# mLSTM scores as 64x64 quadrants, k in 128 rows, and one PSUM bank for all logits

## The chip, the cores and the metric

The kernel runs on one core of one Trainium2 chip. The metric is the device time of one execution in microseconds. Matmuls run on TensorE (PE, with PEld for the loads of its weights), elementwise work on VectorE (DVE), ScalarE (ACT) and GpSimd (POOL), and most DMAs are issued by SyncE (SP). A matmul writes PSUM, which has 8 banks of 512 float32 columns in 128 rows.

## The reference

An mLSTM layer with 4 batches, 8 heads, 768 positions and head size 40 gives x; a mixture of 8 experts, top 1, is applied to x. Everything is float32.

```python
for t in range(S):                      # C: [B,H,40,40], n: [B,H,40], m: [B,H]
    m_new  = max(f[t] + m, i[t])
    f_s, i_s = exp(f[t] + m - m_new), exp(i[t] - m_new);  m = m_new
    C = f_s * C + i_s * outer(v[t], k[t]);  n = f_s * n + i_s * k[t]
    y[t] = sigmoid(o[t]) * (C @ q[t]) / max(abs(n . q[t]), 1)
x = y as [3072 tokens, 320]
logits = normalize(x) @ normalize(expert_emb).T / tau
e, gate = argmax(logits), softmax(logits)[argmax]
out = gate * (relu(x @ w1[e]) @ w2[e])  # w1: [8,320,1024], w2: [8,1024,320]
```

## The kernel before

The recurrence is computed in chunks of L = 64 positions. One step n of the main loop (line 1290, NS = 24 steps) takes one batch and P = 128 positions, two chunks c, for all 8 heads. The heads are split as 4 pairs (index a, NP = 4) of two (index r). A chunk needs its scores (k against q, masked), the state that it starts from, and the product of scores and values. Loads of q, k and the rows of k and v come for two steps at a time (a pair q of steps, NS // 2 = 12 pairs, NB = 3 buffers).

In step n of the loop, TensorE gets its work in this order: `stage_add(n, 0)` (L664 adds the old state by an identity matrix, L674 adds the first chunk's keys times values); `stage_scores(n + 1)` (L637); now and then part of the routing; `stage_y(n)` (L712 scores times values, L725 q times state, and between them in odd steps the five transposes of L792); `stage_add(n, 1)`; in odd steps the router's logits of two steps (L812, two matmuls of 2 x E = 16 columns for each of 5 blocks of 64 features). ScalarE copies the state in the middle of the step from PSUM to `c_mid` in `stage_mid` (L690), which stands right behind `stage_add(n, 0)`. The state in PSUM and y share one bank: `pcv` and `yv` are two parts of the tile `y`. VectorE masks the scores of step n + 1 in `stage_weigh` (L646), and POOL scales the values in `stage_uv` (L622).

The scores of a step are 2 chunks x 4 pairs x 2 heads = 16 products of k and q over 40 rows, each issued as two matmul instructions. q has the even pair's 40 rows in partitions 0 to 39 and the odd pair's in 64 to 103, zeros between. k has two tiles: `k_e` holds the even pairs in the lower half and zeros in the upper, `k_o` the odd pairs in the upper half and zeros in the lower. Each product runs over all 128 rows; the zeros take the other pair out. The zeros are written once per buffer: by VectorE and POOL for buffer 0 (L1095, 1096, 1103, 1109), by ScalarE in `zero_act` (L1087) for buffers 1 and 2. The two heads r of a pair go to the two halves of PSUM's rows, r * 64; all scores of a step fill one bank (tile `s`, pool `pS`).

Loads are issued on SP's queue in the order of the loop: in an even step `stage_k` for a whole pair (two DMAs of 40 rows, L601), in an odd step `stage_q` for a whole pair (one of 128 rows, L607), each followed by `stage_row` (L595) and `stage_sig` (L615), from step 10 on by loads of the first experts' weights (`raw`, L173 to L184), and at the end of the step by the store of x of an earlier step (`x_d`, L766). In some steps ScalarE rounds a piece of those weights (L197), between its other work.

The router works on three groups of steps, GROUPS = (0, 6), (6, 14), (14, 24). Each group has its own PSUM tile `pm`, of the pool `pM` with two buffers. In it lie the logits, the ranks of the tokens within each expert (`pmv(g, 1)`), the sums that give the lists of tokens (`pids`) and counts (`cntv`). The order of the routing is the table `ROUTE` (line 1038); its VectorE parts wait in `vq` and are taken out one at a time by `tick`.

PSUM in the loop: pX 1 bank, pM 2, pY 3, pS 1, pJ 1. After the loop the banks of pY, pS and pJ go to the experts' pools pH and pO; the first experts' x is transposed by `x_tile` into banks of pS and pM, and `x_chunk` takes turns between pM and pX. The order of all work is written out by hand (`manual_schedule`).

Of the kernel before, what the change touches and what calls it, by code (L numbers as in the profile page):

```python
# [11 lines left out]
F32 = mybir.dt.float32  # L12
# [11 lines left out]
E, F = 8, 1024  # L24
# [42 lines left out]
def tile_mlstm_moe(  # L67
# [148 lines left out]
    pX = mctx.enter_context(tc.tile_pool(name="pX", bufs=1, space=PSUM))  # L216
    pM = mctx.enter_context(tc.tile_pool(name="pM", bufs=2, space=PSUM))

# [88 lines left out]
    pp, banks = [], []  # L307
    turns = [(pM, "pm"), (pX, "px")]

# [228 lines left out]
    with ExitStack() as actx:  # L538
# [6 lines left out]
        ap = ictx.enter_context(tc.tile_pool(name="ap", bufs=2, side="right"))  # L545
        pS = ictx.enter_context(tc.tile_pool(name="pS", bufs=1, space=PSUM, side="right"))
        pJ = ictx.enter_context(tc.tile_pool(name="pJ", bufs=1, space=PSUM, side="right"))


# [22 lines left out]

        k_e, k_o, q_s, kv_s, kr_s, vr_s, uv, w_s = [], [], [], [], [], [], [], []
        for i in range(NB):
            k_e.append(ap1.tile([P, 2, NP, P], F32, name=f"k_e{i}"))
            k_o.append(ap1.tile([P, 2, NP, P], F32, name=f"k_o{i}"))
            q_s.append(ap1.tile([P, 2, NP, P], F32, name=f"q_s{i}"))
            kv_s.append(ap1.tile([P, 2, 2, NP, D + D1], F32, name=f"kv_s{i}"))
            kr_s.append(kv_s[i][:, :, :, :, 0:D])
            vr_s.append(kv_s[i][:, :, :, :, D:])  # L580
            uv.append(ap1.tile([P, 2, NP, 2, D1], F32, name=f"uv{i}"))
            w_s.append(ap1.tile([P, 2, NP, L], F32, name=f"w_s{i}"))
        c_st = [ap1.tile([P, NP, 2 * D1], F32, name=f"c_st{b}") for b in range(B)]
# [15 lines left out]
        def stage_k(q, ks=slice(0, 2)):  # L599
            for r, kk in ((0, k_e), (1, k_o)):  # L600
                SY.dma_start(  # L601
                    kk[q % NB][r * L : r * L + D, ks].rearrange("d n a t -> d (n a t)"),
                    kt[q, r][:, ks].rearrange("d n a t -> d (n a t)"),
                )

# [23 lines left out]
        def stage_scores(n):  # L629
            q, k = divmod(n, 2)  # L630
            s = st.setdefault(n, {})["s"] = pS.tile([P, 2, NP, L], F32, name=f"s_{n}", tag="ps")
            for c in range(2):
                cs = slice(c * L, c * L + L)
                for a in range(NP):
                    for r in range(2):
                        m = a // 2 * 2 + r
                        T.matmul(  # L637
                            s[r * L : r * L + L, c, a],
                            (k_e, k_o)[a % 2][q % NB][:, k, m, cs],
                            q_s[q % NB][:, k, m, cs],  # L640
                            start=True,
                            stop=True,
                        )

        def stage_weigh(n):
            V.tensor_tensor(  # L646
                w_s[n % NB].rearrange("p c a t -> p (c a) t"),
                st[n]["s"].rearrange("p c a t -> p (c a) t"),
                late.unsqueeze(1).broadcast_to([P, 2 * NP, L]),
                ALU.mult,  # L650
            )
# [53 lines left out]
        def stage_y(n, mid=None):  # L705

            q, k = divmod(n, 2)
            y = st[n]["y"]
            yp = y[:, 0 : H * D1].rearrange("p (a q r d) -> p a q r d", a=NP // 2, q=2, r=2)
            for a in range(NP):  # L710
                for c in range(2):
                    T.matmul(  # L712
                        y[c * L : c * L + L, a * 2 * D1 : (a + 1) * 2 * D1],
                        w_s[n % NB][:, c, a],
                        uv[n % NB][:, c, a].rearrange("p r d -> p (r d)"),
                        start=False,
                        stop=n < B and c == 0,
                        skip_group_check=True,
                    )
            if mid:  # L720
                mid()
            for m in range(NP):
                for c, state in ((0, c_st[n % B]), (1, c_mid[n % 2])):
                    if n >= B or c:
                        T.matmul(  # L725
                            yp[c * L : c * L + L, m // 2, :, m % 2],
                            q_s[q % NB][:, k, m, c * L : c * L + L],
                            state[:, m].rearrange("p (q d) -> p q d", q=2),
                            start=False,
                            stop=True,  # L730
                            skip_group_check=True,
                        )
# [68 lines left out]
        def stage_logits(q):  # L801
# [3 lines left out]
            b = n - GROUPS[g][0]  # L805
            if b == 0:
                grp[g] = dict(pm=pM.tile([P, 512], F32, name=f"pm_{g}", tag="pm"))
            xt = st.pop(n)["xt"]
            st.pop(n + 1)
            for c in range(NX):  # L810
                for r0 in (0, L):
                    T.matmul(  # L812
                        grp[g]["pm"][r0 : r0 + L, b * E : (b + 2) * E],
                        xt[:, c, r0 : r0 + L],
# [21 lines left out]

        def pmv(g, k):
            w = nt(g) * E
            return grp[g]["pm"][:, k * w : (k + 1) * w].rearrange("p (t e) -> p t e", e=E)

        def pids(g):
            return grp[g]["pm"][:, 2 * nt(g) * E : 2 * nt(g) * E + E * NTT]

# [3 lines left out]
        def route_a(g, n0=0, n1=None):  # L847
# [3 lines left out]
            mx = sm(g, f"mx{n0}", [P, n])  # L851
            pl = pmv(g, 0)[:, n0:n1]
            V.tensor_reduce(mx, pl, AX.X, ALU.max)
# [72 lines left out]
        def route_rank(g):  # L926

            n, rkp, oh = nt(g), pmv(g, 1), ohg(g)
            T.matmul(rkp, tri, oh, start=True, stop=False)
# [6 lines left out]
        def route_b(g):  # L936
# [3 lines left out]
            ro = sm(g, "ro", [P, n, E])  # L940
            V.tensor_tensor(ro, pmv(g, 1), oh, ALU.mult)
            yield
# [61 lines left out]
        def cntv(g):  # L1004
            return grp[g]["pm"][:, 3 * P : 3 * P + E]

# [74 lines left out]

        def flat(t):
            return t.rearrange("p n a t -> p (n a t)")

        def zero_act(t):

            A.activation(  # L1087
                flat(t).rearrange("p (g t) -> p g t", t=P),
                onef.unsqueeze(1).broadcast_to([P, 2 * NP, P]),
                AF.Copy,  # L1090
                scale=0.0,
            )

        fill(FILLS[0])
        V.memset(k_e[0][:, 0], 0.0)  # L1095
        G.memset(k_o[0][:, 0], 0.0)
        stage_gates(1, A)
# [4 lines left out]
        V.memset(onef, 1.0)  # L1102
        V.memset(k_e[0][:, 1], 0.0)
        V.memset(ones[:, 1:], 1.0)
# [3 lines left out]
        G.memset(c_mid[0], 0.0)  # L1108
        G.memset(k_o[0][:, 1], 0.0)
        G.memset(uv[1], 0.0)  # L1110
        G.memset(c_mid[1], 0.0)
        zero_act(k_e[1])
        stage_k(0, slice(1, 2))
# [17 lines left out]
        A.activation(u0, gi[0:NH, 0], AF.Exp, bias=na0)  # L1131
        zero_act(k_o[1])
        fill(FILLS[1])
# [127 lines left out]
        def embeddings(k):  # L1261
# [3 lines left out]
            elif k == 1:  # L1265
# [4 lines left out]
                V.tensor_scalar(en, en, ens, taub[:E], ALU.mult, ALU.mult)  # L1270
                zrow = flat(k_e[2])[P - 1 : P]
                SY.dma_start(x_d[PAD : PAD + 1], zrow[:, 0:DM])
# [17 lines left out]
        for n in range(NS):  # L1290
            last = n == NS - 1
            q = (n + 4 - n % 2) // 2
            if n and q < NS // 2:
                (stage_q if n % 2 else stage_k)(q)
            if q < NS // 2:
# [189 lines left out]
        work(1, 0)  # L1485
        stage_xts(n // 2, pM, "pm")
        do(1)
# [4 lines left out]
        double(xs_a[:, 1], 0, HALF)  # L1492
        x_tile(xa[1], xs_a[:, 1], 0, pM, "pm")
        stage_sq(n - 1)
# [96 lines left out]
    hs = hidden("b")  # L1591
    banks += [(pH, "ph")] * 2 + [(pM, "pm")] * 2
    for e in range(NE):
# [212 lines left out]
def _layout(q, k, v, i_gate, f_gate, o_gate, moe_expert_emb, moe_tau, moe_w1, moe_w2):  # L1806
# [24 lines left out]
    def by_token(a):  # L1831
# [38 lines left out]
```

## Time and profile before

| what | us |
|---|---|
| median of 3 runs | 326.04 (324.49 to 328.71) |
| the profiled execution | 328.47 |
| its span, first to last instruction | 326.7 |
| busy in the span: PE / PEld | 307.4 / 290.8 |
| busy in the span: DVE / ACT / POOL | 217.2 / 164.1 / 146.4 |
| scores (L637): matmuls on k_e and on k_o | 2 x 384 instructions, 222 to 223 ns each |
| c_mid (L690) on ACT | 48 copies, 293 ns each |

Times in the profile are microseconds from the start of the span. An instruction's duration on PE includes its way through the array, so two that start close together overlap; what a block costs is read from the start of its first instruction to the start of the next block. The chain of waits goes back from the last instruction to whatever released each piece of work. The loop over the 24 steps fills the first 112 us or so, the experts the rest.

### The profile page before, as it was taken

How to read it: one execution, taken by the hardware profiler on the slowest of the kernel's cores; microseconds unless marked ns; L12 is line 12 of the kernel's file. 1: busy time of each engine (PE TensorE's matmuls, PEld its weight loads, DVE VectorE, ACT ScalarE, POOL GpSimd, SP SyncE). 2: the span in 40 equal slices, each digit the busy share in tenths (PEclk: the TensorE clock that was granted, in tenths of full speed). 3: DMA queues.
4: the chain of work that ended last, by engine and by line, in shares of the span. 5: the costliest groups of instructions: out<-in, count | busy, mean ns of one | idle time of the engine just before them, and what ended most of it. 6: DMA issues, size and time to landing. Idle time of an engine off the chain costs nothing.

```text
span 326.7 us, 9770 instructions
## 1 busy us (share of the span) xinstructions
PE 307.4 (94%) x3769; PEld 290.8 (89%) x3769; DVE 217.2 (66%) x631; ACT 164.1 (50%) x431; POOL 146.4 (45%) x182
## 2 busy tenths in 40 slices
PE   8998999989988879999999999999999999999991
PEld 3787999978876779999999999999999999999990
DVE  5776797897775549796567684574585584766520
ACT  4656556655663695344265463263373463555300
POOL 6659777688784297040635302321251321512121
PEclk9999999999999979999999999999999999999998
DMA  7998797998997523030594964446446465411001
GB/s 228 283 342 252 264 306 238 290 321 272 340 340 219 183 55 113 2 80 3 180 328 168 316 187 134 129 131 191 124 105 247 112 198 198 129 48 42 10 26 33
DMA packets 25101, 58.52 MB, mean 179 GB/s; under 512 B 3707, under 2 KB 10056, under 8 KB 25046
## 3 DMA queue, kind: packets, MB, share of 16 engines
q1 hardware_dynamic: 22166, 48.91, 47.0%
q0 software_dynamic: 2624, 8.48, 8.4%
q8 instruction: 31, 0.51, 0.7%
q10 hardware_dynamic: 256, 0.43, 0.4%
q14 instruction: 24, 0.20, 0.2%
HBM read 49.98 MB, written 8.19 MB: 178 GB/s over the span
## 4 chain that ended last, share of the span: by engine, by line
PE 84%; DVE 4%; DMA 4%; ACT 4%; issue 2%; POOL 1%; POOLq 0%; DVEq 0%; ACTq 0%
PE ph L390 29%; PE po L428 17%; PE s L637 4%; PE po_b L428 4%; PE po_a L428 4%; PE y L712 4%; PE y L674 3%; PE y L725 3%; PE po L415 3%; PE pt L351 2%; PE warm L1078 2%; DMA k_o<-in_kt 2%; PE pm L812 2%; PE px L792 2%; DMA raw<-in_w 2%
## 5 line engine op out<-in xcount | busy, mean ns | idle before, releaser
L447 POOL DMA_INDIRECT out<-ob,ids x20 | 20.3, 1015 | 99.2 <-DVE ob L444 73.7
L622 POOL TENSOR_TENSOR uv<-kv_s,u_t 64x328 f32<-64x328 f32 x47 | 35.3, 751 | 12.7 <-PE y L674 5.4
L428 PE MATMUL po<-w2h,hh 128*128 128x320 f32 x128 | 40.3, 315 | 0.0
L392 ACT ACTIVATE hh<-ph 128x448 fp32r<-128x448 f32 (+2 forms) x48 | 23.7, 493 | 32.7 <-PE ph L390 29.8
L428 PE MATMUL po<-w2h,hl 128*128 128x320 f32 x128 | 39.6, 309 | 0.0
L428 PE MATMUL po<-w2l,hh 128*128 128x320 f32 x128 | 39.5, 309 | 0.0
L394 DVE SCALAR_TENSOR_TENSOR hl<-ph,hh 128x384 fp32r<-128x384 f32 (+1 forms) x48 | 24.5, 511 | 14.6 <-ACT hh L392 12.3
L390 PE MATMUL ph<-xh,w1l 128*128 128x448 f32 (+2 forms) x96 | 32.0, 337 | 0.0
L390 PE MATMUL ph<-xh,w1h 128*128 128x448 f32 (+2 forms) x96 | 32.0, 336 | 0.0
L197 ACT CAST w1h<-raw 128x512 fp32r<-128x512 f32 x48 | 28.9, 616 | 5.4 <-DMA raw<-in_w 4.9
L444 DVE TENSOR_SCALAR ob<-po,gts 128x320 f32<-128x320 f32 x16 | 8.8, 551 | 27.8 <-PE po L428 27.8
L200 DVE TENSOR_TENSOR w2l<-raw,w2h 128x320 fp32r<-128x320 f32 x58 | 26.7, 497 | 0.2
L197 ACT CAST w2h<-raw 128x320 fp32r<-128x320 f32 x64 | 26.1, 461 | 0.0
L637 PE MATMUL s<-q_s,k_e 128*64 128x64 f32 x384 | 24.5, 223 | 1.2 <-DVE w_s L646 1.2
L690 ACT COPY c_mid<-y 40x164 f32<-40x164 f32 x48 | 14.0, 293 | 22.0 <-PE y L674 21.6
L637 PE MATMUL s<-q_s,k_o 128*64 128x64 f32 x384 | 24.5, 222 | 0.5 <-issue 0.5
L390 PE MATMUL ph<-xl,w1h 128*128 128x448 f32 (+2 forms) x96 | 24.6, 337 | 0.0
L312 POOL DMA_INDIRECT xs<-x_d,ids x20 | 21.4, 1070 | 6.9 <-issue 5.5
L200 DVE TENSOR_TENSOR w1l<-raw,w1h 128x512 fp32r<-128x512 f32 x36 | 24.4, 687 | 0.0
L428 PEld LDWEIGHTS po<-w2l,hh 128*128 128x128 f32 x128 | 24.1, 188 | 0.0
L428 PEld LDWEIGHTS po<-w2h,hh 128*128 128x128 f32 x128 | 24.1, 188 | 0.0
L428 PEld LDWEIGHTS po<-w2h,hl 128*128 128x128 f32 x128 | 24.0, 188 | 0.0
(327 smaller groups left out, 922.2 us busy)
## 6 DMA issues: line engine op xcount, KB each, us to landing
raw<-in_w SPq DMA_DIRECT2D x21, 512.0 KB
raw<-in_w SPq DMA_DIRECT2D x32, 320.0 KB
kv_s<-in_rows SPq DMA_DIRECT2D x23, 324.0 KB
q_s<-in_qt SPq DMA_DIRECT2D x11, 512.0 KB
sig<-in_og SPq DMA_DIRECT2D x24, 160.0 KB
x_d<-x SPq DMA_DIRECT2D x24, 160.0 KB
k_e<-in_kt SPq DMA_DIRECT2D x11, 160.0 KB
k_o<-in_kt SPq DMA_DIRECT2D x11, 160.0 KB
```

The source lines that it names most:

```text
L197: A.copy(h, src)
L200: (eng or V).tensor_tensor(lo, src, h.bitcast(F32), ALU.subtract)
L312: G.indirect_dma_start(out=xs[0 : c.shape[0], a, 0:DM], out_offset=None, in_=x_d[0:rows], in_offset=bass.IndirectOffsetOnAxis(ap=c, axis=0 ...
L390: T.matmul(ph, lt, rh, start=i == 0, stop=i == len(ops) - 1)
L392: A.activation(hh, ph, AF.Relu)
L394: V.scalar_tensor_tensor(hl[:, 0:full], ph[:, 0:full], 0.0, hh[:, 0:full].bitcast(F32), ALU.max, ALU.subtract)
L428: T.matmul(po[0 : ts_.stop - ts_.start, 0:DM], lt[f][:, ts_], rh[:, f], start=k == 0, stop=k == len(ops) - 1)
L447: store = G.indirect_dma_start(out=out, out_offset=bass.IndirectOffsetOnAxis(ap=slots, axis=0), in_=ob, in_offset=None, bounds_check=NT - ...
L622: (eng[r] if eng else G).tensor_tensor(uv[n % NB][rows, :, :, r], vr_s[q % NB][rows, k], u_t[rows, j, b].unsqueeze(3).broadcast_to([L, 2, ...
L637: T.matmul(s[r * L : r * L + L, c, a], (k_e, k_o)[a % 2][q % NB][:, k, m, cs], q_s[q % NB][:, k, m, cs], start=True, stop=True,)
L690: A.copy(dst, src)
L712: T.matmul(y[c * L : c * L + L, a * 2 * D1 : (a + 1) * 2 * D1], w_s[n % NB][:, c, a], uv[n % NB][:, c, a].rearrange("p r d -> p (r d)"), s ...
```

## The change

Four things change.

k gets the layout of q: one tile `k_s` of 128 rows with the even pairs in partitions 0 to 39 and the odd ones in 64 to 103, padded with zeros on the host. `k_e`, `k_o`, `zero_act` and all clears of them are gone. The row of zeros that is stored to x_d as padding now comes from `c_mid[0]`.

k and q are loaded for one step at a time, half of the columns of a buffer, both in every step, in place of k in even and q in odd steps.

Each product of the scores runs over the 40 rows of its own pair only, and the four of (pair h, head r) lie in four quadrants of the array: rows h * 64, columns r * 64. The two h write two banks, so `s` and `w_s` get an index h, and `pS` takes two banks.

The groups of the router share one `pm` tile, with the parts of each group one behind the other; the ranks are written over the logits. `pM` has one buffer. At the end of the loop pS is closed and its two banks become pT, for the first two `x_tile`; after the loop a bank of pY becomes pN, which stands in for pM's second bank.

```diff
-    pM = mctx.enter_context(tc.tile_pool(name="pM", bufs=2, space=PSUM))
+    pM = mctx.enter_context(tc.tile_pool(name="pM", bufs=1, space=PSUM))
...
-    turns = [(pM, "pm"), (pX, "px")]
+    turns = [(pX, "px")]
...
-            k_e.append(ap1.tile([P, 2, NP, P], F32, name=f"k_e{i}"))
-            k_o.append(ap1.tile([P, 2, NP, P], F32, name=f"k_o{i}"))
+            k_s.append(ap1.tile([P, 2, NP, P], F32, name=f"k_s{i}"))
...
-            w_s.append(ap1.tile([P, 2, NP, L], F32, name=f"w_s{i}"))
+            w_s.append(ap1.tile([P, 2, 2, NP // 2, L], F32, name=f"w_s{i}"))
...
         def stage_k(q, ks=slice(0, 2)):
-            for r, kk in ((0, k_e), (1, k_o)):
-                SY.dma_start(
-                    kk[q % NB][r * L : r * L + D, ks].rearrange("d n a t -> d (n a t)"),
-                    kt[q, r][:, ks].rearrange("d n a t -> d (n a t)"),
-                )
+            SY.dma_start(
+                k_s[q % NB][:, ks].rearrange("d n a t -> d (n a t)"), kt[q][:, ks].rearrange("d n a t -> d (n a t)")
+            )
...
         def stage_scores(n):
             q, k = divmod(n, 2)
-            s = st.setdefault(n, {})["s"] = pS.tile([P, 2, NP, L], F32, name=f"s_{n}", tag="ps")
+            s = st.setdefault(n, {})["s"] = pS.tile([P, 2, 512], F32, name=f"s_{n}", tag="ps")
+            sv = s[:, :, 0 : NP * L].rearrange("p h (c i t) -> p h c i t", c=2, i=NP // 2)
             for c in range(2):
                 cs = slice(c * L, c * L + L)
-                for a in range(NP):
-                    for r in range(2):
-                        m = a // 2 * 2 + r
-                        T.matmul(
-                            s[r * L : r * L + L, c, a],
-                            (k_e, k_o)[a % 2][q % NB][:, k, m, cs],
-                            q_s[q % NB][:, k, m, cs],
-                            start=True,
-                            stop=True,
-                        )
+                for i in range(NP // 2):
+                    for h in range(2):
+                        rows = slice(h * L, h * L + D)
+                        for r in range(2):
+                            m = i * 2 + r
+                            T.matmul(
+                                sv[r * L : r * L + L, h, c, i],
+                                k_s[q % NB][rows, k, m, cs],
+                                q_s[q % NB][rows, k, m, cs],
+                                start=True,
+                                stop=True,
+                            )
...
         def stage_weigh(n):
             V.tensor_tensor(
-                w_s[n % NB].rearrange("p c a t -> p (c a) t"),
-                st[n]["s"].rearrange("p c a t -> p (c a) t"),
-                late.unsqueeze(1).broadcast_to([P, 2 * NP, L]),
+                w_s[n % NB].rearrange("p h c i t -> p h (c i) t"),
+                st[n]["s"][:, :, 0 : NP * L].rearrange("p h (c t) -> p h c t", t=L),
+                late.unsqueeze(1).unsqueeze(1).broadcast_to([P, 2, NP, L]),
                 ALU.mult,
             )
...
-                        w_s[n % NB][:, c, a],
+                        w_s[n % NB][:, a % 2, c, a // 2],
...
-            if b == 0:
-                grp[g] = dict(pm=pM.tile([P, 512], F32, name=f"pm_{g}", tag="pm"))
+            if not grp:
+                pm = pM.tile([P, 512], F32, name="pm", tag="pm")
+                grp.update({i: dict(pm=pm) for i in range(len(GROUPS))})
...
+        def pmo(g):
+            return sum(nt(i) * E + E * NTT + E for i in range(g))
+
-        def pmv(g, k):
+        def pmv(g):
             w = nt(g) * E
-            return grp[g]["pm"][:, k * w : (k + 1) * w].rearrange("p (t e) -> p t e", e=E)
+            return grp[g]["pm"][:, pmo(g) : pmo(g) + w].rearrange("p (t e) -> p t e", e=E)
...
-            n, rkp, oh = nt(g), pmv(g, 1), ohg(g)
+            n, rkp, oh = nt(g), pmv(g), ohg(g)
...
-        V.memset(k_e[0][:, 0], 0.0)
-        G.memset(k_o[0][:, 0], 0.0)
...
-        zero_act(k_e[1])
...
-        zero_act(k_o[1])
...
-                zrow = flat(k_e[2])[P - 1 : P]
+                zrow = c_mid[0].rearrange("p m d -> p (m d)")[P - 1 : P]
...
             if n and q < NS // 2:
-                (stage_q if n % 2 else stage_k)(q)
+                stage_k(q, slice(n % 2, n % 2 + 1))
+                stage_q(q, slice(n % 2, n % 2 + 1))
...
-                for t in (k_e[2], k_o[2]):
-                    zero_act(t)
-                stage_k(2)
+                stage_k(2, slice(0, 1))
+                stage_q(2, slice(0, 1))
...
             if last:
                 route(n, 0)
+                sctx.close()
+                pT = ictx.enter_context(tc.tile_pool(name="pT", bufs=2, space=PSUM, side="right"))
...
-                x_tile(xa[0], xs_a[:, 0], 0, pS, "ps")
-                x_tile(xa[0], xs_a[:, 0], 1, pM, "pm")
+                x_tile(xa[0], xs_a[:, 0], 0, pT, "pt")
+                x_tile(xa[0], xs_a[:, 0], 1, pT, "pt")
...
+        pN = mctx.enter_context(tc.tile_pool(name="pN", bufs=1, space=PSUM))
+        turns.append((pN, "pn"))
...
-    banks += [(pH, "ph")] * 2 + [(pM, "pm")] * 2
+    banks += [(pH, "ph")] * 2 + [(pM, "pm"), (pN, "pn")]
...
-        kt=dims_first(k),
+        kt=both_heads(dims_first(k)),
```

More of the change, by code (lines that the diff above doesn't have):

```diff
@@ L545, in tile_mlstm_moe @@
         ap = ictx.enter_context(tc.tile_pool(name="ap", bufs=2, side="right"))
-        pS = ictx.enter_context(tc.tile_pool(name="pS", bufs=1, space=PSUM, side="right"))
         pJ = ictx.enter_context(tc.tile_pool(name="pJ", bufs=1, space=PSUM, side="right"))
+        sctx = ExitStack()
+        pS = sctx.enter_context(tc.tile_pool(name="pS", bufs=1, space=PSUM, side="right"))
         rs = ss_all
@@ L571, in tile_mlstm_moe @@
         stage_gates(0)
-        k_e, k_o, q_s, kv_s, kr_s, vr_s, uv, w_s = [], [], [], [], [], [], [], []
+        k_s, q_s, kv_s, kr_s, vr_s, uv, w_s = [], [], [], [], [], [], []
         for i in range(NB):
-            k_e.append(ap1.tile([P, 2, NP, P], F32, name=f"k_e{i}"))
-            k_o.append(ap1.tile([P, 2, NP, P], F32, name=f"k_o{i}"))
+            k_s.append(ap1.tile([P, 2, NP, P], F32, name=f"k_s{i}"))
             q_s.append(ap1.tile([P, 2, NP, P], F32, name=f"q_s{i}"))
@@ L812, in stage_logits @@
                     T.matmul(
-                        grp[g]["pm"][r0 : r0 + L, b * E : (b + 2) * E],
+                        pmv(g)[r0 : r0 + L, b : b + 2].rearrange("p t e -> p (t e)"),
                         xt[:, c, r0 : r0 + L],
@@ L835, in nt @@
             return GROUPS[g][1] - GROUPS[g][0]
-        def pmv(g, k):
+        def pmo(g):
+            return sum(nt(i) * E + E * NTT + E for i in range(g))
+        def pmv(g):
             w = nt(g) * E
-            return grp[g]["pm"][:, k * w : (k + 1) * w].rearrange("p (t e) -> p t e", e=E)
+            return grp[g]["pm"][:, pmo(g) : pmo(g) + w].rearrange("p (t e) -> p t e", e=E)
         def pids(g):
-            return grp[g]["pm"][:, 2 * nt(g) * E : 2 * nt(g) * E + E * NTT]
+            at_ = pmo(g) + nt(g) * E
+            return grp[g]["pm"][:, at_ : at_ + E * NTT]
         def ohg(g):
@@ L851, in route_a @@
             mx = sm(g, f"mx{n0}", [P, n])
-            pl = pmv(g, 0)[:, n0:n1]
+            pl = pmv(g)[:, n0:n1]
             V.tensor_reduce(mx, pl, AX.X, ALU.max)
@@ L940, in route_b @@
             ro = sm(g, "ro", [P, n, E])
-            V.tensor_tensor(ro, pmv(g, 1), oh, ALU.mult)
+            V.tensor_tensor(ro, pmv(g), oh, ALU.mult)
             yield
@@ L1004, in cntv @@
         def cntv(g):
-            return grp[g]["pm"][:, 3 * P : 3 * P + E]
+            at_ = pmo(g + 1) - E
+            return grp[g]["pm"][:, at_ : at_ + E]
         def early_count():
@@ L1080, in fill @@
                 )
[L1082 to L1092, printed above, removed]
         fill(FILLS[0])
-        V.memset(k_e[0][:, 0], 0.0)
-        G.memset(k_o[0][:, 0], 0.0)
         stage_gates(1, A)
@@ L1102, in tile_mlstm_moe @@
         V.memset(onef, 1.0)
-        V.memset(k_e[0][:, 1], 0.0)
         V.memset(ones[:, 1:], 1.0)
@@ L1108, in tile_mlstm_moe @@
         G.memset(c_mid[0], 0.0)
-        G.memset(k_o[0][:, 1], 0.0)
         G.memset(uv[1], 0.0)
         G.memset(c_mid[1], 0.0)
-        zero_act(k_e[1])
         stage_k(0, slice(1, 2))
@@ L1485, in tile_mlstm_moe @@
         work(1, 0)
-        stage_xts(n // 2, pM, "pm")
+        stage_xts(n // 2, pN, "pn")
         do(1)
@@ L1492, in tile_mlstm_moe @@
         double(xs_a[:, 1], 0, HALF)
-        x_tile(xa[1], xs_a[:, 1], 0, pM, "pm")
+        x_tile(xa[1], xs_a[:, 1], 0, pN, "pn")
         stage_sq(n - 1)
```

## The prediction

> **What bounds the kernel now.** I read the page first (its busy times and chain), then three stretches side by side, then the chain of waits in order of time, then the timeline of single steps.
>
> ```profile
> span 326.7 us, 9770 instructions
> ...
> PE 84%; DVE 4%; DMA 4%; ACT 4%; issue 2%; POOL 1%; POOLq 0%; DVEq 0%; ACTq 0%
> ```
>
> The stretches have the columns length, then busy PE, PEld, DVE, ACT, POOL, the clock, the DMA share and GB/s:
>
> ```profile
> 32.00:58.00 26.00, 26.00 (x682) 24.36 (x679) 20.16 (x77) 15.97 (x50) 18.45 (x25) 1.00 0.83 268
> 58.00:96.00 38.00, 35.05 (x896) 32.35 (x895) 31.45 (x102) 23.20 (x69) 30.02 (x35) 1.00 0.97 318
> 112.00:326.00 214.00, 205.52 (x1437) 201.91 (x1437) 133.97 (x341) 97.29 (x234) 68.79 (x66) 0.99 0.42 127
> ```
>
> TensorE carries 84% of the chain. From 112 us on the experts run, with 205.52 of 214 us of matmuls; the change gives them other banks but as many of them, and I cost that part at nothing (should a bank come free late there, the price is one wait of the kind below, some tenths of a microsecond). So the question lies in the 24 recurrence steps before 112 us. Between 32 and 58 us TensorE is busy without a hole, so a shorter score block looks like pure gain there. One step in close-up says otherwise:
>
> ```profile
> 58.30 0.45 PE L674 MATMUL y<-uv,kv_s 128*40 128x82 f32 x8
> ...
> 58.80 0.60 ACT L690 COPY c_mid<-y 40x164 f32<-40x164 f32 x2 [0.52 <-PE y L674]
> ...
> 59.52 0.74 PE L712 MATMUL y<-uv,w_s 128*64 128x82 f32 x16
> ```
>
> From the chain, and from the list of waits (total us, times, longest):
>
> ```profile
> 71.69 0.04 issue
> 71.74 0.28 PE y L712
> ```
>
> ```profile
> PE y L712 <- ACT c_mid L690: 3.2, 5, 1.0
> ```
>
> In program order TensorE does the state matmuls of step n (L674), the scores of step n+1 (L637), then y of step n (L712). ScalarE meanwhile copies the state out of the same y bank (L690), and L712 waits for that copy, as the last row says: 3.2 us in 5 of the steps. In the step shown the copy starts 0.05 us after L674 ends (58.30+0.45), lasts 0.60 and ends at 59.40; with the 0.05 us that a released L712 takes to start (71.69 to 71.74), y could start at 59.45, and it starts at 59.52. The score block is the cover of the copy, and only 0.07 us longer than it.
>
> **The change part by part.** *Scores as quadrants.* The nearest rows are those of the chain for an even and an odd step:
>
> ```profile
> 36.27 0.93 PE s L637 x32
> 37.21 0.57 PE y L712 x16
> 37.78 0.57 PE y L725 x16
> ...
> 40.99 0.59 PE px L792 x4
> 41.68 0.72 PE y L725 x16
> 42.69 0.54 PE pm L812 x20
> ...
> 146.97 0.44 PE pt L351 x4
> ```
>
> And TensorE's own timeline:
>
> ```profile
> 56.55 0.28 PE L725 MATMUL y<-c_st,q_s 128*64 128x82 f32 x1
> 56.56 0.28 PE L725 MATMUL y<-c_mid,q_s 128*64 128x82 f32 x1
> ```
>
> A block is 32 matmuls in 0.93 us, 29 ns each. Already two run at a time: the last two rows start 0.01 us apart, one in each half of the columns. The count stays 32; what changes is that k and q lie in 40 rows of either half, so that four could run at a time: 0.93/2 = 0.47 us. That is the low end. The high end is no gain, 0.93. I take 0.47, since the halves of the columns show that parts of the array that share nothing do run beside one another.
>
> Against it stands the change of shape. Going from 64 columns to 128 and back costs: four transposes take 0.59 in px but 0.44 in pt, where the neighbours have 128 columns too, so 0.15 to enter; the sixteen L725 behind them take 0.72 instead of 0.57, 0.15 to leave. Whether a change from 128 rows to 64 costs the same no row shows: 0 to 0.30 us a step, and I take 0.30, the only price there is. The block is then 0.47+0.30 = 0.77 us. [...]
>
> Either way it ends before the copy does. In an ordinary step y starts 0.07 us earlier and no more, since c_mid is late next. It then also starts from a wait, which costs something again:
>
> ```profile
> 27.60 0.79 PE L712 MATMUL y<-uv,w_s 128*64 128x82 f32 x16 [1.00 <-ACT c_mid L690]
> ```
>
> 0.79 against 0.74 above: 0.05 back. Of the 23 blocks inside the steps 5 wait for c_mid already (the row of waits) and gain nothing. Three early ones have the copy done long before y; the last two of them:
>
> ```profile
> 13.23 0.61 ACT L690 COPY c_mid<-y 40x164 f32<-40x164 f32 x2
> ...
> 21.41 0.61 ACT L690 COPY c_mid<-y 40x164 f32<-40x164 f32 x2 [1.49 <-PE y L674]
> ```
>
> ```profile
> 15.34 0.74 PE L712 MATMUL y<-uv,w_s 128*64 128x82 f32 x16
> ...
> 22.81 0.31 PE L712 MATMUL y<-uv,w_s 128*64 128x82 f32 x4
> ```
>
> These gain 0.93-0.77 = 0.16 each, 0.5 us (0.46 each, 1.4 us, if the change of shape is free). The other 15 gain 15 x (0.07-0.05) = 0.3 us, with bounds 0 and 15 x 0.07 = 1.1.
>
> *Weighing, on VectorE.* As many elements, from two banks; at nothing, between -0.1 and +0.1 us a step beside a VectorE that has 20.16 of 26 us busy. It begins earlier by what the block is shorter, which I count for nothing.
>
> *Loads.* For each pair of steps two loads of 160 KB (k) and one of 512 (q) become four of 256:
>
> ```profile
> q_s<-in_qt SPq DMA_DIRECT2D x11, 512.0 KB
> ...
> k_e<-in_kt SPq DMA_DIRECT2D x11, 160.0 KB
> ```
>
> Then from the chain, ScalarE's timeline and SP's queue:
>
> ```profile
> 58.81 6.43 DMA k_o<-in_kt
> 65.24 0.02 issue
> 65.26 5.17 DMA raw<-in_w
> ```
>
> ```profile
> 70.45 0.62 ACT L197 CAST w1h<-raw 128x512 fp32r<-128x512 f32 x1 [1.11 <-DMA raw<-in_w]
> ```
>
> ```profile
> 63.17 0.39 SPq L607 DMA_DIRECT2D q_s<-in_qt  x1
> ```
>
> That is 4 x 256 - 512 - 2 x 160 = 192 KB more per pair (the host pads k to 128 rows), 2.3 MB over twelve, and one issue more, 0.39 us on SP's queue, ahead of rows, gates, x stores and the first expert's weights (raw), which are queued behind it. It matters where DMA is full: 0.97 busy at 318 GB/s from 58 to 96 us, and there the chain runs through it, from k_o's landing to raw's issue, its cast on ScalarE, the copy of c_mid and y. Steps 12 to 19, four pairs, issue their loads in that stretch: 4 x 192 KB at 318 GB/s = 2.5 us, if all of it is paid. At the other end nothing is paid, and k_o, 160 KB that took 6.43 us to land, is no longer there to be waited for: up to the 1.11 us that ScalarE idled for raw comes back. So -1.1 to +2.5; I take one late issue, +0.4, the nearest row. [...]
>
> *Zeroing k.* Eight clears go (two on DVE, two on POOL, four on ACT). Two of ACT's stand ahead of the copy at 13.23 us; but y waits for the scores, at 15.34, so nothing is gained. The first gates arrive no earlier. At nothing; the cover is the 1.50 us between 13.84 and 15.34.
>
> *One bank for all logits.* Ranks now overwrite logits and the groups share a bank, so a matmul into it may wait for VectorE's reads of another group. The logits come last in a step and the reads early in it: nothing, at worst a wait as long as the copy above, 0.60 us, in four routing steps, +2.4.
>
> **Sum.** -0.5 -0.3 +0.4 = -0.4 us. The profiled execution took 328.47 us, 1.8 beyond its span, and would take 328.1; the median of the runs shown is 326.04, and that becomes 325.6.
>
> **The rivals.**
> (1) *The quadrants do not run four at a time.* Weights have to be loaded for each of the 32, and pm, which streams 16 columns (2 x E) instead of 64, still takes 0.54/20 = 27 ns each; if that is a floor per matmul, a block is 32 x 27 = 0.86, with the change of shape 1.16, and y comes 0.23 us later in the 18 blocks that do not wait anyway: +4.1, with DMA's 0.4 330.5. With no concurrency at all it is 0.93+0.30, +5.4, 331.8. It decides from the point where the block passes the end of the cover, 0.93-0.07 = 0.86 us. For it: scores and pm have nearly the same pace, so the array's stream is not what they share; against it: the independent halves. [...] Chance 0.2.
> (2) *DMA pays in full.* +2.5 between 58 and 96 us in place of +0.4: 327.5. For it the 0.97; against it the 0.83 of 32 to 58 us, where the same pairs are loaded with room. Chance 0.12.
> (3) *c_mid does not hold y, and the change of shape is free.* Then all 18 blocks gain 0.46: -8.3, with DMA's 0.4 318.1. Against it stands the row of waits; for it only that 10 or so steps show no wait as they are. Chance 0.05.
> (4) *The block stays at 0.93*, gain and price cancelling out: with DMA's 0.4 326.4. Chance 0.05, inside the range of the forecast.
> The forecast itself, 0.58: its own range is 322.4 (1.4+1.1 gained in the blocks and 1.1 from DMA) to 328 (the gains lost, half a bank's waits and half of DMA's 2.5 paid).
>
> **The numbers.** Runs of the same kernel spread from 324.49 to 328.71 us, 0.7% either way, and 2% (6.5 us) is about what a measurement of it can tell. The range has to hold the forecast, (2), (4) and most of (1): 321.5 to 331. Faster by over 2% (below 319.5) needs (3): 0.06. Slower by over 2% (above 332.6) needs (1) without concurrency and DMA paid besides: 0.09. The rest, 0.85, is within 2%.
>
> **What would show it.** Right: the scores of a step take 0.47 to 0.8 us instead of 0.93; the waits list L712 on c_mid in about 20 steps instead of 5, each 0.1 to 0.3 us; the distance from L674 to L712 stays at 1.2 us; the stretch from 32 to 58 us, counted in steps, is as long as before. The first L712 behind the scores is spaced as L725 behind px is, if the change of shape costs. Rival 1 shows as scores of 0.86 us or more with L712 right behind them and no wait. Rival 2 shows as a DMA share near 1 and a raw that lands later, with ScalarE's casts waiting for it. The forecast is wrong if y starts less than 0.85 us behind the first score, or if one of the routing matmuls waits for VectorE.

## The result, and the profile after

The changed kernel took 330.75 us (median of 4 runs, 329.79 to 331.54); before took 325.26 beside it (4 runs, 324.07 to 328.71). The ratio is 1.0144, interval 1.010 to 1.0189. Two repeats beside other runs of before gave 1.0135 (1.0069 to 1.0201) and 1.0084 (1.0045 to 1.0123): the change costs about 1%, some 3 to 4 us, where 0.4 us less were forecast. The first four runs of before lay low: 133 of them in all later comparisons, on three chips, have a median of 326.97 (323.33 to 332.51). So only ratios against runs of before taken on the same chip are used below. Now and then an execution falls into a slower state; every ratio goes by the other runs alone, and the profile of bank (below), which was taken in that state, is left out where times of profiles are compared.

The page of the changed kernel: its span, the row of the clock in 40 slices, and the shares of the chain.

```profile
span 328.0 us, 9770 instructions
...
PEclk9996999999999979999999999999999999999999
...
PE 61%; DVE 1%; ACT 1%; issue 0%; POOL 0%; POOLq 0%; ACTq 0%
```

The fourth digit of the clock is new: from 24.6 to 32.8 us the granted clock was 0.6 on average, with 0.50 from 26.3 to 33.1 us. (The chain can be followed back only to the experts here, so its shares don't compare with those of before.) The stretches, in the columns explained above:

```profile
32.00:58.00 26.00, 23.93 (x623) 20.66 (x625) 17.93 (x69) 13.29 (x42) 17.89 (x26) 0.98 0.85 270
58.00:96.00 38.00, 33.60 (x883) 29.04 (x877) 30.01 (x105) 23.54 (x70) 28.27 (x33) 1.00 0.94 310
112.00:328.00 216.00, 206.59 (x1447) 202.79 (x1447) 136.28 (x345) 99.51 (x240) 70.19 (x67) 0.99 0.41 127
```

Between 32 and 58 us TensorE was busy without a hole before; now 2.07 us of 26 are holes, and fewer matmuls are done (x623 for x682); the first 1.1 us still lie in the clock of 0.50. The experts are as they were. One step in close-up, TensorE's timeline and then ScalarE's:

```profile
57.33 0.45 PE L675 MATMUL y<-uv,kv_s 128*40 128x82 f32 x8
57.71 0.69 PE L638 MATMUL s<-q_s,k_s 40*64 40x64 f32 x32
58.47 0.79 PE L713 MATMUL y<-uv,w_s 128*64 128x82 f32 x16
```

```profile
57.83 0.60 ACT L691 COPY c_mid<-y 40x164 f32<-40x164 f32 x2 [1.42 <-PE y L675]
```

Of the groups of instructions between 28 and 109 us, the scores (busy, mean ns of one, idle time before them):

```profile
L638 PE MATMUL s<-q_s,k_s 40*64 40x64 f32 x576 | 13.1, 225 | 1.8 <-issue 1.8
```

The 32 score matmuls last 0.69 us to the end of the last, which alone takes 0.225, so their starts spread over 0.47 us, half of the 0.93 of before, where two run at a time: four run at a time. c_mid ends at 58.43 and y starts 0.04 later. From L675 to y it is 1.14 us, against 1.22 before.

What the change of shape costs can be read from these rows and from an early step in which c_mid was done long before. Before and then after:

```profile
14.36 0.34 PE L637 MATMUL s<-q_s,k_e 128*64 128x64 f32 x4
...
58.30 0.45 PE L674 MATMUL y<-uv,kv_s 128*40 128x82 f32 x8
58.59 0.28 PE L637 MATMUL s<-q_s,k_e 128*64 128x64 f32 x4
```

```profile
13.86 0.69 PE L638 MATMUL s<-q_s,k_s 40*64 40x64 f32 x32
14.48 0.79 PE L713 MATMUL y<-uv,w_s 128*64 128x82 f32 x16
```

From the first L675 to the first score it is 0.38 us (57.33 to 57.71), where it was 0.29: about 0.1 us to enter. From the first score to y it is 0.62 us where c_mid holds nothing, 0.15 more than the 0.47 of the scores' starts; before it was 0.98 (14.36 to 15.34), 0.05 more than the 0.93 over which the scores' starts spread in that step: about 0.1 us to leave. So the change of shape costs 0.2 us a step.

And the waits (total us, times, longest), before and then after:

```profile
ACT w1h L197 <- DMA raw<-in_w: 4.9, 5, 1.8
...
PEld y L712 <- ACT c_mid L690: 3.9, 5, 1.1
```

```profile
PEld y L713 <- ACT c_mid L691: 8.2, 18, 1.5
...
ACT w1h L197 <- DMA raw<-in_w: 7.2, 6, 1.9
...
PE y L713 <- ACT c_mid L691: 4.8, 6, 1.4
```

y's weights (PEld) now wait for c_mid in 18 steps instead of 5. Its matmuls (PE) are listed in 6: in the other steps the last score, whose 0.225 us are still running, covers most of the wait. Step by step, the y of step 4 starts at 26.79 us (27.60 before), that of step 5 at 34.00 (32.67), that of step 23 at 109.16 (106.92). From there to the end it takes 218.8 us (219.8 before). So 0.8 us is gained up to step 4, 3.0 are lost between there and step 23, and 1.0 comes back behind it. Of the 3.0, 2.1 lie between steps 4 and 5, where the clock is low.

### The profile page after: what moved, and what is told of

The parts are those of the page before. It is cut to its first block, busy times and chain, and to the rows that moved or that the text cites. A ratio compares the mean times of both kernels' runs of the same rounds, so it can differ in the third digit from the quotient of the medians.

```text
span 328.0 us, 9770 instructions
## 1 busy us (share of the span) xinstructions
PE 304.8 (93%) x3768; PEld 284.2 (87%) x3769; DVE 216.4 (66%) x629; ACT 161.0 (49%) x427; POOL 145.1 (44%) x180
## 4 chain that ended last, share of the span: by engine, by line
PE 61%; DVE 1%; ACT 1%; issue 0%; POOL 0%; POOLq 0%; ACTq 0%
PE ph L390 29%; PE po L428 17%; PE po_b L428 4%; PE po_a L428 4%; PE po L415 3%; PE pt L351 2%; DVE w2l L200 1%; ACT w1h L197 1%; PE pg L519 0%; DVE hl_a L394 0%; POOL out L447 0%; PE px L793 0%; PE pa L366 0%; ACT xt L799 0%; DVE ob L444 0%
## 5 line engine op out<-in xcount | busy, mean ns | idle before, releaser
L394 DVE SCALAR_TENSOR_TENSOR hl<-ph,hh 128x384 fp32r<-128x384 f32 (+1 forms) x48 | 24.6, 513 | 14.8 <-ACT hh L392 14.7
L200 DVE TENSOR_TENSOR w2l<-raw,w2h 128x320 fp32r<-128x320 f32 x58 | 26.3, 491 | 0.2
L713 PE MATMUL y<-uv,w_s 128*64 128x82 f32 x384 | 19.9, 246 | 5.7 <-ACT c_mid L691 4.8
L390 PE MATMUL ph<-xl,w1h 128*128 128x448 f32 (+2 forms) x96 | 24.6, 337 | 0.0
L713 PEld LDWEIGHTS y<-uv,w_s 128*64 128x64 f32 x384 | 15.7, 140 | 8.7 <-ACT c_mid L691 8.2
```

Source lines behind the costliest of these rows:

```text
L200: (eng or V).tensor_tensor(lo, src, h.bitcast(F32), ALU.subtract)
L390: T.matmul(ph, lt, rh, start=i == 0, stop=i == len(ops) - 1)
L394: V.scalar_tensor_tensor(hl[:, 0:full], ph[:, 0:full], 0.0, hh[:, 0:full].bitcast(F32), ALU.max, ALU.subtract)
L713: T.matmul(y[c * L : c * L + L, a * 2 * D1 : (a + 1) * 2 * D1], w_s[n % NB][:, a % 2, c, a // 2], uv[n % NB][:, c, a].rearrange("p r d -> ...
```

## The experiments

The edits are shortened to the lines that matter.

**The parts of the change, one at a time.** `bank` is before with the shared pm bank alone, the eighth bank as a pool of its own:

```diff
-    pM = ... bufs=2          +    pM = ... bufs=1;  pN = ... bufs=1
-  grp[g] = dict(pm=pM.tile(...))   # one tile per group
+  grp.update({i: dict(pm=pm) for i in range(len(GROUPS))})
```

> The kernel before, with the shared pm bank alone (pM has one buffer; the eighth bank becomes a pool of its own for the late tiles). If the time went to TensorE waiting for VectorE's reads of that bank, this kernel shows all of it: 329 to 331 us. If it went to the quadrants, the loads or the clock of the start, it stays at the 325.3 us of before, within 1 us, and its profile shows how an ordinary execution of the kernel before runs.

Measured: 0.9994 of before (0.996 to 1.0028), clock 0.990. The bank costs nothing that can be told from zero.

`pair` is the changed kernel with whole pairs loaded in the old order, k still padded to 128 rows; `quad` has also k in 40 rows, so that all loads are those of before; `half` is before with half columns.

```diff
 pair   -  stage_k(q, slice(n % 2, n % 2 + 1)); stage_q(q, slice(n % 2, n % 2 + 1))
        +  (stage_q if n % 2 else stage_k)(q)
 quad   +  for r in range(2): SY.dma_start(k_s[q % NB][r * L : r * L + D, ks], kt[q, r][:, ks])
 half   -  (stage_q if n % 2 else stage_k)(q)
        +  stage_k(q, slice(n % 2, n % 2 + 1)); stage_q(q, slice(n % 2, n % 2 + 1))
```

> The changed kernel with the loads of before: a whole pair of steps at a time, k in even and q in odd steps; k still in 128 rows. If the half-column loads (one issue more per pair, k and q of a step arriving together) cost the time, 325 to 327 us. If the quadrants, the bank or the clock do, it stays at 330 to 331 us.

> The changed kernel with all loads of before: whole pairs, k in even and q in odd steps, k in two loads of 40 rows (the quadrants read only these rows). So it is before with the quadrants and the one bank alone. If the loads (padding, or their order) cost the time, 326.5 to 328 us, not above before. If the quadrants cost it (shorter blocks, then a wait, so that TensorE is idle more and its clock falls), 329 us, as with whole pairs and padding.

> The kernel before, loaded for one step at a time (half the columns of k_e, k_o and q in every step), nothing else changed: no byte more, three issues more per pair. If the half-column loads cost the time, 328 to 331 us. If not, 325.3 us within 1 us.

Measured: pair 1.0035 (0.9994 to 1.0076), quad 0.9988 (0.9942 to 1.0034), half 1.0037 (0.9997 to 1.0076). Without the half columns the change costs nothing that can be told from zero, with or without padding. On the kernel before, the half columns are not told from zero either.

`again`, run beside quad, and `again2`, run beside `pair2`, are the changed kernel once more; pair2 is pair once more. With the latter two ran `narrow`: the changed kernel with its half columns, but k in two loads of 40 rows, without the padded bytes.

> Once more the changed kernel with whole pairs and padding (1.0035 of before, interval 0.9994 to 1.0076), to be set beside the changed kernel on the same chip: if the half columns cost 1% by themselves, 1.003 to 1.006 against 1.0135; if the two are the same, both at 1.006 to 1.012.

> The changed kernel as it is, once more, beside the others. Before has a mean of 327.9 us over 34 runs here, more than the 325.3 of its first four, so part of the 4.7 us may be chance. If the change costs what its first four runs say, 330 to 331 us and a mean clock of 0.976; if most of it was chance, 328 to 329 us and a clock near the 0.989 of before.

> The changed kernel, a third time, as the partner of the others on this chip: 1.010 to 1.017 of before by the two comparisons so far (1.0144 and 1.0135), and another trace in which to see whether the clock falls to half near 27 us (it did in both so far).

> The changed kernel with k's half columns loaded in 40 rows (two loads of 80 KB per step in place of one of 256 KB with padding): its bytes are those of before, its loads are three per step and smaller. If the padded bytes cost the time, 0.999 to 1.004 of before. If the number of loads does (each has to wait for an earlier one on SP's queue), 1.01 or more.

Measured: pair2 0.9994 (0.9958 to 1.003); again 1.0135 and again2 1.0084, as above; narrow 1.0079 (1.0047 to 1.0111). The intervals of pair2 and again2, which ran together, lie apart: in the changed kernel the cost comes with the half-column loads, and it stays when the padded bytes go.

**Bytes by themselves, a measurement that missed its aim.** `pad` is before with k's two loads of 64 rows in place of 40.

```diff
-  kk[q % NB][r * L : r * L + D, ks]     # 40 rows
+  kk[q % NB][r * L : r * L + L, ks]     # 64 rows, zeros from the host
```

> The kernel before, with k's two loads of 64 rows instead of 40, zeros from the host in the others: the 192 KB more per pair of the change, nothing else. If the added bytes cost the time, 329 to 330.5 us (up to 2.5 us, 0.77 MB at 318 GB/s, for the four pairs between 58 and 96 us). If not, 328 us within 0.7.

Measured: 1.031 (1.0243 to 1.0376), 10 us, four times the bound. It is not the price of bytes, since pair and pair2 move as many at 1.0035 and 0.9994. The chain of pad:

```profile
13.38 7.77 DMA k_o<-in_kt
...
21.17 8.25 DMA sig<-in_og
```

A load of k takes 7.77 us to land, a sigmoid input waits for its landing to be issued, and c_mid and y of step 4 wait for that: y of step 4 starts at 32.17 (27.60 before), which is 4.6 of the 10 us. SP's queue, pad and then pair2:

```profile
39.88 0.55 SPq L601 DMA_DIRECT2D k_o<-in_kt  x1
```

```profile
41.51 0.38 SPq L600 DMA_DIRECT2D k_s<-in_kt  x1
```

The issue of 64 rows took 0.55 us, that of 128 rows with twice the bytes 0.38. So pad says that this form of load is bad in this kernel, not why, and it isn't in the change.

**The clock.** `fills` adds six matmuls, whose results nobody reads, in step 4, where TensorE waits for the embeddings and for c_mid; `keep` adds two behind the scores of every step from the third on; `qfills` is quad with the six.

```diff
 fills  +  fill(2); embeddings(2); fill(4)                    # n == 4
 keep   +  T.matmul(st[n + 1]["s"][:, h, 256:512], ones..., ones...)   # h = 0, 1
```

> The changed kernel with six matmuls more in step 4, whose results nobody reads, in the two holes in which TensorE waits for the embeddings and for c_mid (0.56 and 0.99 us in the profile after). If the time goes to the half clock that TensorE got from 26.3 to 33.1 us there, the clock stays at full speed up to 100 us and the time falls by the 2 us that y lost between steps 4 and 5: 328 to 329 us. If the clock is not what costs, 330.5 to 331.5 us.

> The changed kernel with two matmuls of 128x256 behind the scores of every step from the third on, written to unused columns, where TensorE waits for c_mid. If the half-speed windows of the clock cost the time, the mean clock rises from 0.976 to 0.985 or more and the time falls to 328 to 329 us. If the cost is elsewhere, the time stays at 330.5 us or rises by what the matmuls cost where nothing waits, up to 24 x 0.2 = 5 us.

> Quadrants and one bank with all loads of before (k in 40 rows, whole pairs: 0.9988 of before), plus the six matmuls in the holes of step 4 (which took the changed kernel from 1.0135 to 1.0071). If the half-speed clock between 26 and 33 us is a cost that the quadrants bring by arriving early at step 4, the two effects add: 0.992 to 0.996 of before, some 2 us faster than before. If the six matmuls only cover a loss that the loads bring, it stays at 0.999, or rises by what six matmuls cost (1.3 us, 1.003).

Measured: fills 1.0071 (1.0033 to 1.0109) with a mean clock of 0.984, keep 1.0074 (1.0032 to 1.0115) with 0.986, where the changed kernel has 0.976 to 0.978 and before 0.988 to 0.989. In neither profile does the clock fall near 27 us; it falls once later in the loop (fills at 104.4, keep at 66.4 us). The intervals of both overlap those of the changed kernel. qfills 0.9986 (0.9947 to 1.0025): no gain over quad. What the clock does is seen in step 4 and behind it, again2 and then pair2:

```profile
24.00:26.50 2.50, 1.32 (x52) 1.09 (x52) 2.27 (x9) 1.70 (x6) 2.50 (x4) 0.99 0.73 261
26.50:33.30 6.80, 6.43 (x77) 5.64 (x77) 2.81 (x14) 3.04 (x11) 4.32 (x16) 0.50 0.98 300
```

```profile
24.00:26.50 2.50, 2.30 (x74) 2.03 (x68) 2.24 (x10) 1.71 (x6) 2.50 (x4) 1.00 0.44 153
26.50:33.30 6.80, 5.73 (x130) 4.95 (x130) 4.18 (x17) 3.76 (x13) 5.45 (x17) 1.00 0.95 309
```

In again2 TensorE is busy 1.32 of 2.50 us; then the clock is 0.50 for 6.8 us, in which 77 matmuls are done. At full clock pair2 does 130. The two waits of again2 in that stretch:

```profile
PE y L713 <- ACT c_mid L691: 1.0, 1, 1.0
PE pen L1266 <- DVE en L1259: 0.6, 1, 0.6
```

The first is there in before as well. The second is new: TensorE comes to the embeddings 0.6 us before VectorE has them ready; in before it came to them at 25.85 us, 0.7 later than here, and did not wait. The clock falls at 26.3 in the changed kernel and at 26.5 in again2, with 0.5 and 0.6 us of the wait for c_mid gone by. From y of step 4 to that of step 5 it is 7.2 us in these two, 5.0 in pair2 and qfills: a fall of 6.8 us costs 2.2. The four profiles of the changed kernel and narrow all show a fall between 26 and 28 us (6.8 or 3.4 us long; one of 3.4 us costs 0.8); of quad, pair and pair2, with whole pairs, one does (quad, 3.4 us), and half, without the quadrants, does not. In the changed kernel and again2 the clock fell when TensorE had been idle for 1.05 and 1.15 of the last 1.8 and 1.9 us, in two pieces of 0.5 to 0.6 us. Such holes are not followed by a fall each time: before has 1.22 us of holes at 95 to 98.6 us, pad one hole of 1.84 us at 74.8, and their clock stays at 1.00. What makes the clock fall is not shown by these profiles, only that two holes of 0.5 to 0.6 us went ahead of both falls of 6.8 us near 27 us.

So with the added matmuls of fills and keep the clock is higher, while the time falls from 1.012 (the mean of the three ratios of the change) to 1.007, less than the intervals can tell; and the two of keep in each step are work themselves.

The clock of every run is on record, not only that of the profiled ones. Means over the runs that the ratios go by; the last column is an estimate from them, 2 x (1 - clock) x span, since the profiles show only the clocks 1.00 and 0.50:

```
                                    mean clock        us at half clock per run
before (five comparisons)           0.988 to 0.989    7 to 8
bank, half                          0.990             6
quad, qfills, pair, pair2           0.985 to 0.988    8 to 10
fills, keep                         0.984, 0.986      10, 9
joint2k, jfills (below)             0.982             12
after, again, again2, narrow        0.976 to 0.978    14 to 16
joint, split (below)                0.978, 0.979      15, 14
ahead, ahead_b (further below)      0.981, 0.989      12, 7
```

The kernels that lose most have 6 to 9 us more at half clock than before. If TensorE had work in all of it, that would cost half of this by the same estimate, 3 to 4 us, all of the loss. Among the runs of one kernel, though, 0.01 of clock goes with 1.5 us (one slope through all kernels' runs, each about its own mean), half of the full price. By these two measures the clock goes with between half and all of the loss. That is a correlation and not a strict one: joint2k and jfills have the same clock and lose 0.7 and 1.4%, and ahead (below) loses nothing at 0.981.

**What it is in the loads.** Four kernels between whole pairs and half columns. `joint`: k and q side by side in one tile, one load of 512 KB per step. `joint2k`: the same, but k and q apart, rows of two pieces of 2 KB. `split`: four loads of 256 KB per pair in the old order. `jfills`: joint with the six matmuls.

```diff
 joint  -  stage_k(q, half); stage_q(q, half)
        +  SY.dma_start(kq_s[q % NB][:, k], kqt[q][:, k])       # k and q of one step
 split  +  for h in range(2): (stage_q if n % 2 else stage_k)(q, slice(h, h + 1))
```

> The changed kernel with k and q side by side in one tile, loaded for one step at a time in one load of 512 KB with rows of 4 KB: k and q of a step together as in the change, the same bytes, but half as many loads. If the number of loads or their short rows cost the time, 0.998 to 1.003 of before. If it is that k and q of one step come together, 1.008 to 1.014 as the change.

> The same in one load of 512 KB, but k and q lie apart, so that each row is two pieces of 2 KB. If the number of loads costs, 0.998 to 1.003 of before; if the short rows cost, 1.006 to 1.014.

> The changed kernel with its four loads of 256 KB per pair in the order of before: both halves of k in even steps, both of q in odd ones. If the number or the short rows cost the time, 1.008 to 1.014 of before as the change; if it is that k and q of one step come together, 0.999 to 1.004.

> The joint loads with the six matmuls in the holes of step 4. If these keep the clock up where the changed kernel lost it (mean clock 0.977 with half columns, 0.985 with the matmuls), and the joint loads cost nothing, 0.994 to 0.999 of before, the shortest of all; if the matmuls hide only a loss of the half-column loads, the same as the joint loads alone.

Measured: joint 1.014 (1.0078 to 1.0202), joint2k 1.007 (1.0038 to 1.0102), split 1.0142 (1.0088 to 1.0195), jfills 1.0139 (1.0082 to 1.0195). No single one of the three explanations stands: joint has few loads and long rows, split has the old order, and both are as slow as the change. joint2k, with 0.7%, lies between. What the profiles of the slower ones show are stalls of TensorE in the middle of a block, as here in split:

```profile
49.69 0.30 PE L675 MATMUL y<-uv,kv_s 128*40 128x82 f32 x3
51.25 0.37 PE L675 MATMUL y<-uv,kv_s 128*40 128x82 f32 x5 [1.26 <-issue]
```

Eight equal matmuls, and between the third and the fourth 1.26 us in which nothing is waited for that the profile shows. In the DMA view of the 1.2 us before that (48.8 to 50.0) there is a packet on a queue of instructions:

```profile
q1 hardware_dynamic: 218, 0.43, 97.9%
q8 instruction: 1, 0.02, 5.1%
```

One packet of 16 KB of instructions, landed at 49.86. TensorE goes on 1.39 us later. In the 20 profiles of this study, between 27 and 108 us, every stall of this kind of 0.5 us or more, 47 of them, ends 1.2 to 1.6 us after the landing of such a packet; 14 or 15 packets land in the 81 us. That the packets are TensorE's program and that it waits for them is the author's inference from these times: the profile does not name their engine. Nor is it shown that the data on q1 (97.9% of 16 engines' time in this view) make them late: a packet took 0.95 us in the median ahead of a stall, and 0.97 where none followed (240 packets).

**Where TensorE's time goes.** From the y of step 4 to that of step 23, per profile: length; TensorE's holes, of them stalls and waits for c_mid; half of the time at half clock; the rest, which is its work. Means over the profiles of a group:

```
                                         length  holes  (stalls, c_mid)  clock   work
before, half                              78.5    5.5     2.0    2.4      0.0    73.0
whole pairs: quad, qfills, pair, pair2    78.1    6.6     2.7    1.9      1.7    69.8
per step: after, again, again2, narrow    80.4    7.8     2.5    3.4      3.3    69.4
joint, joint2k, split, jfills             80.4    8.6     5.4    1.0      1.7    70.1
```

By these means the quadrants take some 3 us of work from TensorE. (A wait that the last score still covers counts as work.) With whole pairs the clock and the holes take most of it back. In the other groups all of it goes, and more: to the clock and c_mid with loads per step, to stalls with the joint and split ones. But these are single executions, and two of one kernel differ by more than the groups do: pair took 81.1 and pair2 76.8 us; the changed kernel 82.4, 77.6 (again) and 82.7 (again2). Above all, the profiled executions of joint and split had clocks of 0.987 and 0.986, where their means are 0.978 and 0.979, so the table has too little clock for them. What the groups lose their time to is not shown by it.

**Filling the wait for c_mid.** `ahead` is quad with the five transposes of odd steps (and step 4) ahead of y, and ScalarE's copy that they read ahead of c_mid; `ahead_b` the same on before.

```diff
-  stage_add(n, 0); stage_mid(n); stage_xc(n - 2); ... stage_y(n, turn)
+  stage_add(n, 0); stage_xc(n - 2); stage_mid(n); ... turn(); stage_y(n)
```

> Quadrants and one bank with the loads of before (0.9988), and in odd steps (and step 4) the five transposes put ahead of y instead of into it, where TensorE waits for c_mid; ScalarE writes what they read ahead of c_mid. If the wait for c_mid eats the gain of the quadrants, some 0.2 to 0.3 us come back in each of 10 odd steps and up to 0.7 in step 4: 2 to 3.5 us, 0.988 to 0.993 of before. If TensorE's lost time lies elsewhere (its own stalls in mid-block, the loads), 0.997 to 1.001.

> The same reordering in the kernel before, without quadrants, the bank or the loads. There the score block covers the copy of c_mid to within 0.07 us, so the transposes have nothing to fill but step 4: 0.996 to 1.001 of before by the theory that c_mid's wait takes the quadrants' gain. If the reordering helps by itself, as much as with the quadrants.

Measured: ahead 0.9985 (0.9947 to 1.0024), ahead_b 0.9967 (0.9922 to 1.0013). The order gives quad nothing that can be told from zero. TensorE's waits in ahead between the y of steps 4 and 23:

```profile
PE y L715 <- ACT c_mid L693: 3.9, 5, 0.9
PE px L795 <- ACT xc L788: 2.1, 3, 0.8
```

The waits for c_mid are still there, and those for the copy put ahead of it (xc) have joined them. So the wait moved, and whether c_mid was what took the gain stays open. No version here is told apart from before on the fast side.

## Why the prediction was wrong

The range, 321.5 to 331.0, holds 330.75 by luck: its upper end was there for rival 1, which did not happen. The number and its sign do not hold. By the steps:

- *The experts, at nothing*: right (205.52 of 214 us of matmuls before, 206.59 of 216 after).
- *Scores as quadrants, 0.47 us, four at a time*: right, 0.47. *The change of shape, 0.30*: it costs, but 0.2: 0.1 to enter and 0.1 to leave. The three early blocks, priced at a gain of 0.16 us each, gave 0.36 (0.98 to 0.62), because no price of entering shows there: two start behind a wait, and at 13.86 us the first score starts 0.07 us before the warm-up matmuls end, as at 14.36 us in before. The y of step 4, which waits for c_mid, comes 0.8 us earlier, where 0.5 was forecast.
- *c_mid holds y*: right for the step (18 waits of y's weights, about 20 forecast; 1.14 us from L675 to y, 1.2 forecast; y then takes 0.79). The sign that was to refute it, y less than 0.85 us behind the first score, did appear (57.71 to 58.47 is 0.76), yet y starts 0.04 us after c_mid: the 0.1 us of entering stands ahead of the first score, which the sign had not allowed for. *So the gain is 0.8 us*: quad's interval is -1.9 to +1.1 us, which neither shows nor excludes it.
- *One bank*: right, at nothing. A routing matmul does wait for VectorE, the other sign, but for 0.5 us as in before.
- *Zeroing k, at nothing*: not contradicted. The y of step 0 does start at 9.84 us instead of 10.39, but 0.35 of this is the shorter block of scores in front of it (from 9.21; before from 9.41), and 0.2 are VectorE's first gates, which come 0.3 earlier in half as well, where all clears are kept. What the working left out is where the earlier arrival leads: to the hole at the embeddings in step 4.
- *Loads, +0.4 in -1.1 to +2.5*: the step that failed. It priced bytes (192 KB per pair) and one issue. The bytes cost nothing that can be told from zero (pair 1.0035 and pair2 0.9994, beside 0.9988 of quad). The form of the loads, which the working counted as one issue of 0.39 us, costs about 1%: 0.7 to 1.4% in every version of the change that loads by the step or in halves, -0.1 to 0.35% with whole pairs.
- *TensorE's speed* was no term at all. Of what is late next the working names c_mid only; the falls of the clock (2.2 us for one of 6.8 us) and TensorE's stalls that end 1.2 to 1.6 us after a packet of instructions has landed stand in no step.
- *Rival 1* gave the measured number, 330.5, by a mechanism that is refuted: the quadrants do run four at a time, their matmuls 15 ns apart on average, below the 27 ns of pm that this rival took for a floor. *Rival 2*, DMA in full, had the right part and the wrong place: raw is waited for longer (7.2 us, 4.9 before), but the DMA share between 58 and 96 us is 0.94, not higher than before (0.97). *Rivals 3 and 4* fall with the scores of 0.47 us. Two sums are slips that decide nothing: rival 2 comes to 327.7, not 327.5, and the upper end of the forecast's own range to 328.5, not 328.

Open is why loading by the step costs 1%: number, row length and order were each excluded as the only cause. What the kernels that lose 0.79% or more share is a lower mean clock (0.976 to 0.982, before 0.988 to 0.989). Whether it is the cause of half or all of the loss, or its companion, no run here decides: raising it with added matmuls (fills, keep, jfills) did not bring back the time of before, and ahead has a clock of 0.981 without a loss.

## What to carry to other kernels

Here work was taken from TensorE where the wait for c_mid was only 0.07 us away, and in the step in close-up y came 0.08 us earlier (1.14 for 1.22 us). In step 4 TensorE came to the embeddings 0.7 us earlier and had holes of 0.5 to 0.6 us there and at c_mid, and in two profiles the clock was 0.50 for 6.8 us behind them; so price the holes as well. Where a kernel's DMA is as busy as here (0.94 to 0.97 from 58 to 96 us), test the form of its loads apart from their bytes: the same bytes cost nothing, 1% or 3% in different loads. And take several runs of the kernel before next to each variant: its first four lay 1.7 us below the median of the later ones. Read the clock of all runs, too, before an explanation is built on the profiled one: that of joint and split was not typical.

## What the runs showed of the hardware that was not expected

- In the changed kernel and again2 the clock fell to half for 6.8 us when TensorE had been idle for 1.05 and 1.15 of the last 1.8 and 1.9 us, in two pieces; a single hole of 1.0 us at the same place in before was not followed by a fall (clock 1.00 from 24 to 33 us).
- Scores in four quadrants start 15 ns apart on average (32 in 0.47 us), where two halves gave 29 (32 in 0.93); in this kernel a change from 128 rows to 40 and back cost about 0.1 us each way (0.38 us from the first L675 to the first score for 0.29, and 0.15 us between the scores and y for 0.05).
- On the queue q8 of instructions packets of 16 KB land, 14 or 15 between 27 and 108 us, and all 47 unexplained stalls of TensorE there of 0.5 us or more end 1.2 to 1.6 us after one lands.
- A load of 64 rows and 256 KB took 0.55 us of SP's queue (pad), one of 128 rows and 512 KB 0.38 (pair2).
